# Placing TensorE's side jobs between score fills by the time that ScalarE has in hand

## The chip, the cores and the metric

The kernel runs on one core of a Trainium2 chip. The time is that of one execution on the device, in microseconds (us); the median of several executions stands for a kernel. The engines of a core are TensorE (matmuls, PE in the profile), VectorE (DVE), ScalarE (ACT), GpSimd (POOL) and SyncE (SP), which here only issues transfers.

## The reference

The input x has 2048 positions of 512 features, in bf16. Two attentions with 32 heads of 16 features run on it and are mixed by a gate for each position:

```python
def reference(A_x, A_wqkv, A_wo, B_x, B_wqkv, B_wo, gate_w):
    x = A_x
    g = sigmoid((x * gate_w).sum(-1, keepdims=True))
    a = A_ref(x, A_wqkv, A_wo)   # softmax(q k^T / 4) v over all 2048 keys, then wo
    b = B_ref(x, B_wqkv, B_wo)   # each position sees 8 keys: itself and every second one before it
    return g * a + (1 - g) * b
```

The full attention needs 32 x 2048 x 2048 exponentials, some 134 million. This is what fills the time.

## The kernel before, in words

**Tiles and periods.** The full attention is cut into 32 periods. A period is one chunk of 512 queries for one group of four heads. Within it there are 64 units: one head, 512 queries and one tile of 128 keys. A unit is a matmul of scores (128 keys x 512 queries, one PSUM bank), 65,536 exponentials, and a matmul of the result with V (17 rows, the last of which gives the sum for the softmax) into the accumulator `acc`.

**Where the exponentials are done.** Most units go to ScalarE, in sets that use two PSUM rings in turn: ring A holds three units, ring B two. TensorE fills a ring with scores (`act_stream`, inner `f`: the *fill*, matmuls `ring<-qt,kt_all`), ScalarE turns the whole ring into probabilities with one instruction (`act_tail`: `pT<-ring`), which frees the ring for the fill after next, and TensorE then multiplies by V (`pv_job`: `acc<-pT,vp_all`, called a *V block* here). A fill may carry one or two more units, for which `rider` takes a *job bank* `w`: VectorE computes their exponential with a polynomial in four passes (`dve_unit`: `ta<-w`, twice `ta<-ta,w`, `pd<-ta,w`), or it copies them out and GpSimd computes it (`pool_unit`, tiles `psc`). `idle_fill` can also place such a unit alone, by `solo`.

**Jobs.** All else that TensorE does goes into the two job banks too: projections for queries, keys and values (`q_job`, `k_job`, `kpk_job`, `qpk_job`, `v_job`), the projections and transposes of the sliding attention (`b_proj`, `b_attn`, whose arithmetic is on GpSimd), transposes of finished accumulators (`post_job`, `ot_job`) and the output projections (`final_job`). Most are four matmuls of 512 columns. For 24 of the 32 periods the queries go by way of memory: `qpk_job` projects them, VectorE and GpSimd finish them, a transfer writes them, and `q_read` reads them back two periods ahead of use.

**The order.** The program is written by a planner, class `Plan`, while the kernel is built. It keeps a clock for each engine (`free`), a list of work that is ready (`ready`, with priority, earliest start, the generator, duration, function, bank needed, and in place 7 the time at which it became ready) and the free slots of banks and buffers. It always takes the engine that can start first, and of that engine's ready work that with the lowest priority number: fills have 0, V blocks just over 1, jobs from 2 on. What it picks is issued at once, so the planner's order is the order of each engine's instructions; each engine then runs in order, and only semaphores decide the times. The planner's durations are constants in the code (`MM` 0.22, `SW` 0.11 and `VP` 0.60 us, and 0.050 + 0.4267 us a unit for ScalarE).

**What holds a job back.** A job that would start at `st` must pass `fits`. It does so if it ends before ScalarE, by the planner's clock, has worked off what is ready for it, less a margin `refill`, or if it has waited longer than `patience`:

```python
        if x[0] < 2 or st - x[7] > self.patience or self.spent:
            return True
        lim = max(self.free["act"], st) + sum(y[4] for y in self.ready["act"]) - self.refill
        return st + x[4] <= lim or self.free["act"] + 3.0 < st
```

A set gets into `ready["act"]` only once `act_tail` has a probability buffer (`pTA` and `pTB`, two of each). `rider` gives VectorE no second unit (`flying`) while a job with a near due time is ready.

**Filler.** Where TensorE would be idle for long, `fill_pass` adds matmuls with zero weights, which add zero (`acc<-ident,z`), and a fill may be written twice (*doubled fill*), so that TensorE stays active.

All instructions are recorded through one wrapper, so nearly all carry its line, L292, and are told apart by their tiles.

Of the kernel before, what the change touches and what calls it, by code (L numbers as in the profile page):

```python
# [51 lines left out]
class Plan:  # L52
# [13 lines left out]
    held = {"job": 0}  # L66
    streamed = deque()
    cap_job = 2
    refill = 0.56
    patience = 6.0  # L70

    def resource(self, name, n):
# [97 lines left out]
    def gate(self, need):  # L170
# [6 lines left out]
            return None  # L177
        return min(x[0] for x in self.slots[need])

    def fits(self, x, st):  # L180

        if x[0] < 2 or st - x[7] > self.patience or self.spent:
            return True
        lim = max(self.free["act"], st) + sum(y[4] for y in self.ready["act"]) - self.refill
        return st + x[4] <= lim or self.free["act"] + 3.0 < st

    def run(self):
        while True:
            best = None
            for e, lst in self.ready.items():  # L190
                rs = []
                for x in lst:
                    g_ = self.gate(x[6])
                    if g_ is not None:
                        rs.append(max(x[2], g_))
                if rs:
                    st = max(self.free[e], min(rs))
                    if best is None or st < best[0]:
                        best = (st, 1, e)
            for r, lst in self.reqs.items():  # L200
                if lst and self.slots[r]:
                    st = max(min(x[0] for x in self.slots[r]), min(x[2] for x in lst))
                    if best is None or st <= best[0]:
                        best = (st, 0, r)
            if best is None:
                return
            st, kind, nm = best
            self.now = st
            if kind == 0:
                lst = self.reqs[nm]  # L210
                x = min(y for y in lst if y[2] <= st + 1e-9)
                lst.remove(x)
                s = min(y for y in self.slots[nm] if y[0] <= st + 1e-9)
                self.slots[nm].remove(s)
                self.advance(x[3], st, s[1])
            else:
                lst = self.ready[nm]
                ok = [y for y in lst if y[2] <= st + 1e-9 and self.gate(y[6]) is not None
                      and self.gate(y[6]) <= st + 1e-9]
                x = min(ok, key=lambda y: (y[0], y[1]))  # L220
                if nm == "pe" and not self.fits(x, st):
                    for y in ok:
                        y[2] = max(y[2], st + 0.1)
                    continue
                lst.remove(x)
                if nm == "pe":
                    self.idle_fill(st, 1 + (x[6] is not None))
                if x[6] is not None:
                    slot = self.take(x[6], st)
                    self.held["job"] += 1  # L230
                    more = x[5](slot)
                else:
                    more = x[5]()
                if isinstance(more, float):
                    x[4] += more
                if nm == "pe":
                    self.stream(st, x[4] - 0.11 - self.thin)
                    self.thin = 0.0
                if CFG_DEBUG:
                    LOG.append((st, x[4], nm, getattr(x[3], '__name__', '?'), x[0]))  # L240
                self.free[nm] = st + x[4]
                self.advance(x[3], st + x[4] + self.LAT[nm], None)
# [3 lines left out]
def kernel(  # L246
# [141 lines left out]
    P = Plan(["pe", "act", "dve", "pool", "sp"])  # L388
# [21 lines left out]
    UR = 0.7  # L410
# [37 lines left out]
    NP = len(periods)  # L448
# [328 lines left out]
    front = [0]  # L777
# [11 lines left out]
    flying = [0]  # L789
# [125 lines left out]
    def act_tail(k, parts, rname, rslot, ring, n):  # L915
        pname = "pTA" if k % 2 == 0 else "pTB"
        pslot = yield ("acq", pname, k)
        st = {}

        def f():  # L920
            st["pT"] = work.tile([128, 3 if k % 2 == 0 else 2, QW], BF16, name="pT", tag=pname, bufs=2)
            A.activation(out=st["pT"][:, 0:n, :], in_=ring[:, 0:n, :], func=ACT.Exp,
                         scale=LN2 / 128.0, bias=-VOFF * LN2 / 128.0)
        yield ("act", k, 0.050 + 0.4267 * n, f)
        yield ("rel", rname, rslot)
        pT = st["pT"]
        off = 0
        for q_, (p, us) in enumerate(parts):
            items = [(t, j, pT[:, off + z, :]) for z, (t, j) in enumerate(us)]
            off += len(us)  # L930
            yield ("spawn", pv_job(p, items, (pname if q_ == len(parts) - 1 else "none", pslot), 1 + 1e-4 * k))

    def act_stream():
        while front[0] < NP:
# [5 lines left out]
            units, parts, used = [], [], []  # L940
# [17 lines left out]
            for p_, us in parts:  # L958
                yield ("wait", ev_q[p_])
                for t, j in us:  # L960
                    yield ("wait", ev_k[periods[p_][1]][t // TPC])
                if ev_start[p_].time is None:
                    yield ("set", ev_start[p_])
            ring = ps.tile([128, 3 if k % 2 == 0 else 2, QW], FP32, tag=rname, bufs=1, name="ring")
            dur = SW + MM

            def f():
# [20 lines left out]
                    ndve[0] += 1  # L988
                return float(more)
            yield ("pe", 0, dur, f)  # L990
            yield ("spawn", act_tail(k, parts, rname, slot, ring, len(units)))
        P.spent = True
        yield ("spawn", end_banks("rA", 3))
# [31 lines left out]
    def rider(js, now=None):  # L1025
        now = P.now if now is None else now
        for p in (front[0], front[0] + 1):
# [5 lines left out]
            if not opts:  # L1033
                continue
            j = max(opts, key=lambda j_: len(pend[p][j_]))
            if flying[0] and any(x[6] and x[0] < 4.0 + 0.3 * min(front[0] + UR, 16.3) for x in P.ready["pe"]):
                return None
            if not P.free_at("w", now):
                return None
# [1 line left out]
            if psc[0] is not None and rem(p) >= PMIN and P.free_at("psc", now):  # L1041
                hs = P.take("psc", now)
                npool[0] += 1
            else:
                if not P.free_at("pd", now) or flying[0] > 1:
                    return None
                flying[0] += 1
                ds = P.take("pd", now)
            act_left[p] -= 1
            act_due[p] -= 1  # L1050
# [3 lines left out]
    def dve_unit(p, t, j, s, ds, wt, n):  # L1054
        lo = wt[:].bitcast(U16).rearrange("p (n two) -> p n two", two=2)[:, :, 0]
        st = {}
        pr = 40 + 1e-3 * n

        def e1():
            st["ta"] = work.tile([128, QW], FP32, name="ta", tag="ta", bufs=2)  # L1060
            V.tensor_scalar(out=st["ta"][:], in0=lo, scalar1=A3, scalar2=None, op0=ALU.mult)

        def e23(a):
            ta = st["ta"]
            V.scalar_tensor_tensor(out=ta[:], in0=ta[:], scalar=a, in1=lo, op0=ALU.add, op1=ALU.mult)
        yield ("dve", pr, VP, e1)
# [1 line left out]
        yield ("dve", pr, VP, lambda: e23(A1))  # L1068

        def e4():  # L1070
            st["pd"] = work.tile([128, QW], BF16, name="pd", tag=f"pd{ds}", bufs=1)
            V.scalar_tensor_tensor(out=st["pd"][:].bitcast(U16), in0=st["ta"][:], scalar=A0 - VOFF / 2.0,
                                   in1=wt[:], op0=ALU.add, op1=ALU.add)
# [553 lines left out]
```

## Time and profile before

| | |
|---|---|
| median of 11 runs | 867.49 us (865.93 to 871.87) |
| profiled execution | 865.93 us, of it 864.1 us from the first to the last instruction |
| ScalarE | 835.8 us busy (97%) |
| TensorE matmuls | 753.3 us (87%), weight loads 267.8 us beside them |
| VectorE, GpSimd | 751.1 us and 750.4 us (87% each) |
| `pT<-ring` on ScalarE | 721 instructions, 823.3 us busy, 12.6 us idle before them |
| units on VectorE and GpSimd | 224 and 22 of 2048 |
| first and last exponential | start at 19.17 us, end at 854.26 us |

A row of the profile names the engine, the operation, the tiles written and read with their shapes, the count, the busy time and the mean length of one in ns, and last the idle time of the engine ahead of it with what ended that. The busy time of a group is a union: instructions that overlap are counted once. TensorE's records overlap, since matmuls are pipelined.

### The profile page before, as it was taken

The page shows a single profiled execution, that of the slowest core. Times are in us where ns is not written, and L with a number is a line of the kernel's source. Part 1 is how long each engine was busy: PE and PEld are TensorE (multiplying, and loading weights), DVE is VectorE, ACT ScalarE, POOL GpSimd, SP SyncE. Part 2 cuts the span into 40 slices and gives each one's busy share as a digit, 9 for nine tenths or more (in the row PEclk, how much of TensorE's full clock was granted, in tenths as well). Part 3 has the DMA queues.
Part 4 walks back from the last instruction along what each step waited for, and adds up shares of the span by engine and source line. Part 5 has one row for each costly group of instructions (what it writes and reads, how often), then busy time and mean ns, then how long its engine had stood idle before and what let it go on. Part 6 is the DMA issues. An engine that isn't in the chain of part 4 may idle for free.

```text
span 864.1 us, 16034 instructions
## 1 busy us (share of the span) xinstructions
PE 753.3 (87%) x5977; PEld 267.8 (31%) x6038; DVE 751.1 (87%) x1312; ACT 835.8 (97%) x753; POOL 750.4 (87%) x758
## 2 busy tenths in 40 slices
PE   8898998898988888888898998888888988888887
PEld 4333342243223333332323232323232323223222
DVE  5696889999999989989999889889988889998884
ACT  5999999999999999999999999999999999999996
POOL 2586995999898989999999999998989999978883
PEclk9999999999999999999999999999999999999999
DMA  9000424422215131221042322303022230010000
GB/s 293 2 2 25 136 62 121 147 69 88 96 55 172 31 111 50 80 68 42 7 136 61 92 73 75 104 8 111 1 62 68 84 124 7 25 45 7 1 2 25
DMA packets 55712, 59.79 MB, mean 69 GB/s; under 512 B 3649, under 2 KB 52289, under 8 KB 55633
## 3 DMA queue, kind: packets, MB, share of 16 engines
q1 hardware_dynamic: 54816, 58.50, 21.5%
q8 instruction: 47, 0.77, 0.4%
q10 hardware_dynamic: 816, 0.26, 0.1%
q14 instruction: 33, 0.26, 0.1%
HBM read 46.14 MB, written 12.62 MB: 68 GB/s over the span
## 4 chain that ended last, share of the span: by engine, by line
ACT 51%; issue 20%; PE 18%; DVE 9%; POOL 1%; another core or an unknown queue 0%; ACTq 0%; DVEq 0%; POOLq 0%
ACT pT L292 50%; PE w L292 6%; PE ring L292 6%; PE acc L292 5%; DVE ta L292 4%; DVE pd L292 1%; POOL psc L292 1%; ACT lg L292 1%; DVE kpk L292 1%; PE last L292 1%; PE heat L292 1%; DVE kmax_pk L292 1%; PE xt L292 0%; DVE crow L292 0%; ACT xT L292 0%
## 5 line engine op out<-in xcount | busy, mean ns | idle before, releaser
L292 ACT ACTIVATE pT<-ring 128x1536 bf16<-128x1536 f32 (+1 forms) x721 | 823.3, 1308 | 12.6 <-PE ring L292 8.2
L292 PE MATMUL ring<-qt,kt_all 32*128 32x512 bf16 x1874 | 289.5, 382 | 92.6 <-ACT pT L292 79.8
L292 DVE SCALAR_TENSOR_TENSOR ta<-ta,w 128x512 f32<-128x512 f32 x448 | 297.8, 682 | 5.9
L292 POOL TENSOR_TENSOR prod<-prod 128x512 f32<-128x512 f32 (+1 forms) x208 | 240.1, 1166 | 6.0
L292 PE MATMUL acc<-pT,vp_all 128*17 128x512 bf16 x1802 | 224.6, 384 | 0.1
L292 PEld LDWEIGHTS <-kt_all 32*128 32x128 bf16 x2120 | 107.0, 91 | 335.2 <-issue 317.6
L292 DVE TENSOR_SCALAR ta<-w 128x512 f32<-128x512 uint16 x224 | 151.6, 685 | 37.5 <-PE w L292 36.7
L292 PE MATMUL acc<-ident,z 128*32 128x512 bf16 (+4 forms) x717 | 161.3, 338 | 2.0 <-DVE accS L292 1.8
L292 DVE SCALAR_TENSOR_TENSOR pd<-ta,w 128x512 uint16<-128x512 f32 x224 | 150.8, 680 | 2.7
L292 POOL TENSOR_TENSOR prod<-ksh,qb 128x512 f32<-128x512 bf16 x128 | 145.0, 1156 | 2.1
L292 POOL TENSOR_TENSOR prod<-vsh,lg 128x512 f32<-128x512 bf16 x128 | 136.6, 1098 | 2.4
L292 PE MATMUL w<-qt,kt_all 32*128 32x512 bf16 x246 | 89.9, 383 | 0.1
L292 POOL TENSOR_TENSOR psc<-psc 128x512 f32<-128x512 f32 x66 | 78.8, 1193 | 5.2
L292 PE MATMUL acc<-pd,vp_all 128*17 128x512 bf16 x246 | 80.2, 383 | 0.0
L292 PEld LDWEIGHTS <-z 128*32 128x32 bf16 x742 | 49.7, 95 | 76.3 <-issue 58.4
L292 PEld LDWEIGHTS <-vp_all 128*17 128x17 bf16 x2048 | 43.8, 88 | 85.2 <-issue 82.4
L292 POOL TENSOR_SCALAR psc<-psc 128x512 f32<-128x512 uint16 (+1 forms) x44 | 27.2, 619 | 34.0 <-DVE psc L292 31.1
L292 PE MATMUL w<-bw,xT 128*128 128x512 bf16 x161 | 47.5, 381 | 3.3 <-issue 0.5
L292 PEld LDWEIGHTS <-xT 128*128 128x128 bf16 x512 | 31.2, 97 | 34.7 <-issue 22.3
L292 POOL TENSOR_TENSOR lg<-lg,mx 128x256 f32<-128x256 f32 x16 | 10.1, 629 | 23.2 <-DVE mx L292 23.2
L292 DVE CAST kvs<-w 128x512 bf16<-128x512 f32 x32 | 22.0, 686 | 5.8 <-PE w L292 5.8
L292 DVE COPY accS<-acc 128x512 f32<-128x512 f32 (+1 forms) x32 | 21.6, 675 | 4.4 <-ACT accS L292 4.0
(115 smaller groups left out, 494.1 us busy)
## 6 DMA issues: line engine op xcount, KB each, us to landing
ksh<-kv_scr SPq DMA_DIRECT2D x16, 1024.0 KB
vsh<-kv_scr SPq DMA_DIRECT2D x16, 1024.0 KB
kv_scr<-kvs SPq DMA_DIRECT2D x16, 256.0 KB
kt_all<-k_scr SPq DMA_DIRECT2D x6, 512.0 KB
q_scr<-qpk SPq DMA_DIRECT2D x24, 128.0 KB
qt<-q_scr SPq DMA_DIRECT2D x24, 128.0 KB
xr<-in_A_x_dram SPq DMA_DIRECT2D x4, 512.0 KB
out_dram<-osb SPq DMA_DIRECT2D x14, 128.0 KB
```

Of the source, the lines that this page charges most:

```text
L292: return chain_on(self._key, f(*a, **k))
```

## The change

`fits` no longer lets a job through because of its age. The limit moves to a function of its own, `limit`, which also counts `coming`: the planned ScalarE time of sets that are filled and whose `act_tail` still waits for a probability buffer (added after a fill is issued, taken off when the buffer is had). `refill` goes from 0.56 to 0.5. A job that has waited over `CALM` = 4 us may pass the limit by `RAMP` = 0.02 of the wait beyond that.

In all periods but the first and the last (`calm`) a job for a job bank is put off by 0.1 us at a time, up to `JP` = 3 us, while VectorE has less than `JW` = 1.6 us of work: what it has begun, the queued work of jobs, and 0.6 us for each pass of a unit still to come (`passes`). In `rider` a ready job keeps a second unit from VectorE only if VectorE has that much work. `feed_dve` and the branch on `DEFER` are added with `HUNG` = 0 and `DEFER` = 0.

```diff
--- before.py
+++ after.py
@@ -66,7 +66,7 @@
     held = {"job": 0}
     streamed = deque()
     cap_job = 2
-    refill = 0.56
+    refill = 0.5
     patience = 6.0
 
     def resource(self, name, n):
@@ -177,12 +177,47 @@
             return None
         return min(x[0] for x in self.slots[need])
 
+    DEFER = 0.0
+    coming = 0.0
+    RAMP = 0.02
+    CALM = 4.0
+
+    def limit(self, st):
+        return max(self.free["act"], st) + sum(y[4] for y in self.ready["act"]) + self.coming - self.refill
+
+    passes = 0
+    calm = False
+    JW = 1.6
+    JP = 3.0
+    HUNG = 0.0
+    ASL = 1.2
+
+    def dve_work(self, st):
+
+        return (max(0.0, self.free["dve"] - st) + 0.6 * self.passes
+                + sum(y[4] for y in self.ready["dve"] if y[0] < 40))
+
+    def room_for_job(self, x, st):
+        return not self.calm or st - x[7] > self.JP or self.dve_work(st) >= self.JW
+
+    def feed_dve(self, st):
+
+        if self.solo is None or not self.calm or self.dve_work(st) >= self.HUNG:
+            return False
+        if max(0.0, self.free["act"] - st) + sum(y[4] for y in self.ready["act"]) + self.coming < self.ASL:
+            return False
+        at = self.solo(self.free["pe"], st + 0.35)
+        if at is None:
+            return False
+        self.stream(at, 0.22)
+        self.free["pe"] = at + 0.33
+        return True
+
     def fits(self, x, st):
 
-        if x[0] < 2 or st - x[7] > self.patience or self.spent:
+        if x[0] < 2 or self.spent or self.free["act"] + 3.0 < st:
             return True
-        lim = max(self.free["act"], st) + sum(y[4] for y in self.ready["act"]) - self.refill
-        return st + x[4] <= lim or self.free["act"] + 3.0 < st
+        return st + x[4] - self.limit(st) <= max(0.0, self.RAMP * (st - x[7] - self.CALM))
 
     def run(self):
         while True:
@@ -218,6 +253,18 @@
                 ok = [y for y in lst if y[2] <= st + 1e-9 and self.gate(y[6]) is not None
                       and self.gate(y[6]) <= st + 1e-9]
                 x = min(ok, key=lambda y: (y[0], y[1]))
+                if nm == "pe" and 1 <= x[0] < 1.5 and st - x[2] < self.DEFER:
+                    jobs = [y for y in lst if y[0] >= 2 and y[4] > 0.5 and y[7] <= st
+                            and self.gate(y[6]) is not None and self.gate(y[6]) <= st + 1e-9]
+                    y = min(jobs, key=lambda y: (y[0], y[1])) if jobs else None
+                    if (y is not None and st + y[4] <= self.limit(st)
+                            and (y[6] != "w" or self.room_for_job(y, st))):
+                        x = y
+                if nm == "pe" and self.feed_dve(st):
+                    continue
+                if nm == "pe" and x[6] == "w" and not self.room_for_job(x, st):
+                    x[2] = max(x[2], st + 0.1)
+                    continue
                 if nm == "pe" and not self.fits(x, st):
                     for y in ok:
                         y[2] = max(y[2], st + 0.1)
@@ -915,6 +962,7 @@
     def act_tail(k, parts, rname, rslot, ring, n):
         pname = "pTA" if k % 2 == 0 else "pTB"
         pslot = yield ("acq", pname, k)
+        P.coming -= 0.050 + 0.4267 * n
         st = {}
 
         def f():
@@ -960,6 +1008,7 @@
                 for t, j in us:
                     yield ("wait", ev_k[periods[p_][1]][t // TPC])
                 if ev_start[p_].time is None:
+                    P.calm = 0 < p_ < NP - 1
                     yield ("set", ev_start[p_])
             ring = ps.tile([128, 3 if k % 2 == 0 else 2, QW], FP32, tag=rname, bufs=1, name="ring")
             dur = SW + MM
@@ -988,6 +1037,7 @@
                     ndve[0] += 1
                 return float(more)
             yield ("pe", 0, dur, f)
+            P.coming += 0.050 + 0.4267 * len(units)
             yield ("spawn", act_tail(k, parts, rname, slot, ring, len(units)))
         P.spent = True
         yield ("spawn", end_banks("rA", 3))
@@ -1033,7 +1083,7 @@
             if not opts:
                 continue
             j = max(opts, key=lambda j_: len(pend[p][j_]))
-            if flying[0] and any(x[6] and x[0] < 4.0 + 0.3 * min(front[0] + UR, 16.3) for x in P.ready["pe"]):
+            if flying[0] and (not P.calm or P.dve_work(now) >= P.JW) and any(x[6] and x[0] < 4.0 + 0.3 * min(front[0] + UR, 16.3) for x in P.ready["pe"]):
                 return None
             if not P.free_at("w", now):
                 return None
@@ -1045,6 +1095,7 @@
                 if not P.free_at("pd", now) or flying[0] > 1:
                     return None
                 flying[0] += 1
+                P.passes += 4
                 ds = P.take("pd", now)
             act_left[p] -= 1
             act_due[p] -= 1
@@ -1057,10 +1108,12 @@
         pr = 40 + 1e-3 * n
 
         def e1():
+            P.passes -= 1
             st["ta"] = work.tile([128, QW], FP32, name="ta", tag="ta", bufs=2)
             V.tensor_scalar(out=st["ta"][:], in0=lo, scalar1=A3, scalar2=None, op0=ALU.mult)
 
         def e23(a):
+            P.passes -= 1
             ta = st["ta"]
             V.scalar_tensor_tensor(out=ta[:], in0=ta[:], scalar=a, in1=lo, op0=ALU.add, op1=ALU.mult)
         yield ("dve", pr, VP, e1)
@@ -1068,6 +1121,7 @@
         yield ("dve", pr, VP, lambda: e23(A1))
 
         def e4():
+            P.passes -= 1
             st["pd"] = work.tile([128, QW], BF16, name="pd", tag=f"pd{ds}", bufs=1)
             V.scalar_tensor_tensor(out=st["pd"][:].bitcast(U16), in0=st["ta"][:], scalar=A0 - VOFF / 2.0,
                                    in1=wt[:], op0=ALU.add, op1=ALU.add)
```

## The prediction

> **What bounds the kernel now.** I read the page's busy shares first, then ScalarE's group row, then its waits, then its busy time by stage, and at last one waiting place in the timeline. The busy shares name the engine:
>
> ```profile
> span 864.1 us, 16034 instructions
> PE 753.3 (87%) x5977; PEld 267.8 (31%) x6038; DVE 751.1 (87%) x1312; ACT 835.8 (97%) x753; POOL 750.4 (87%) x758
> ACT 51%; issue 20%; PE 18%; DVE 9%; POOL 1%; another core or an unknown queue 0%; ACTq 0%; DVEq 0%; POOLq 0%
> L292 ACT ACTIVATE pT<-ring 128x1536 bf16<-128x1536 f32 (+1 forms) x721 | 823.3, 1308 | 12.6 <-PE ring L292 8.2
> L292 PE MATMUL ring<-qt,kt_all 32*128 32x512 bf16 x1874 | 289.5, 382 | 92.6 <-ACT pT L292 79.8
> ```
>
> ScalarE is busy 97% of the span, nearly all of it in 721 exponentials of score sets. The last row shows that TensorE, on the whole, waits for ScalarE (79.8 us), so there is room on TensorE; but ScalarE also waits for TensorE, 12.6 us ahead of those exponentials. By form they are 360 of 1536 columns (mean 1.520 us) and 361 of 1024 (1.098 us); that sums to 942.9 us against 823.3 us of busy time, so neighbours overlap by 119.6 / 720 = 0.166 us. A gap costs its idle time and that overlap. By stage (the columns are TensorE, weight loads, VectorE, ScalarE, GpSimd):
>
> ```profile
> 100.00:200.00 100.00, 90.53 (x746) 35.58 (x755) 90.55 (x160) 98.06 (x89) 86.66 (x89) 1.00 0.32 96
> ...
> 200.00:300.00 100.00, 87.87 (x681) 30.07 (x684) 92.00 (x163) 98.25 (x88) 92.62 (x90) 1.00 0.29 94
> ...
> 700.00:800.00 100.00, 84.31 (x687) 29.21 (x686) 92.47 (x161) 99.01 (x90) 87.92 (x87) 0.98 0.13 41
> ```
>
> Over all stretches from 20 to 830 us ScalarE is idle 810.00 - 800.38 = 9.62 us. Its timeline has 41 gaps over 60 ns there. So all that better placing of TensorE's work can win is 9.6 + 41 x 0.166 = 16.4 us, 1.9%. What makes a gap is seen at 466 us:
>
> ```profile
> 464.22 0.60 PE L292 MATMUL acc<-pT,vp_all 128*17 128x512 bf16 x5
> ...
> 464.76 1.04 PE L292 MATMUL w<-bwo,obt 128*128 128x512 bf16 x4
> ...
> 465.73 0.39 PE L292 MATMUL ring<-qt,kt_all 32*128 32x512 bf16 x3
> ...
> 466.23 1.45 ACT L292 ACTIVATE pT<-ring 128x1536 bf16<-128x1536 f32 x1 [0.50 <-PE ring L292]
> ```
>
> A probability-times-V block (0.54 us from 464.22 to 464.76), then a job of four matmuls (0.97 us to 465.73), and only then the score fill, which ScalarE has been waiting for; the exponential starts 0.50 us after its fill. Of the 41 gaps, 35 (7.0 of 9.4 us that they sum to) have such a job just ahead of the late fill. That is what the planner's `fits` is to prevent.
>
> **What the Trainium skill says.** ScalarE: Activation LUTs, "What ACT_TABLE_LOAD costs", gives an ACTIVATE 186 or 280 ns (immediate or pointer bias) plus 0.833 ns a column, so 1466 or 1560 ns at 1536; the trace has 1520, in between. It lets neighbours overlap by about 93 ns; the trace has 166, which I use. PSUM — Partial Sum Buffer, "Specifications (TRN2)", gives 8 banks of 512 FP32 values; the program's two rings (3 + 2), two job banks and one accumulator use all 8, so no third ring can absorb a late fill, and a fill must come in the time of one exponential. The trace agrees in that fills wait for ScalarE 244 times. TensorE: Matmul & The Clock Gate, "What's actually happening", has the clock at half rate after an idle window of about 3.4 us. The trace shows a dip to 0.66 at 620 to 625 us and at 743 to 748 us, and in each one gap (0.58, 0.76 us) in which plain fills were slow, not jobs.
>
> **The change part by part.** All is decided when the program is built; what reaches the chip is another order, which can be counted in the two programs.
>
> *Rule for jobs* (`limit`, `fits`). Before, a job that had waited 6 us went in whatever it delayed; after, it may exceed the limit by 2% of its wait beyond 4 us, 0.04 us at 6 us. In return `coming` adds sets whose fill is issued and which wait for a probability buffer, and the margin falls from 0.56 to 0.50, so jobs are also allowed sooner. I count the work between one score fill and the next in TensorE's order, each block at its traced time (job 0.97, V blocks 0.32 to 0.54). Gaps with over 1.3 us: 46 before, 15 after (0.33). Neighbouring gaps with over 2.0 us together: 56 and 18 (0.32). Gaps with a full job and a V block: 37 and 17 (0.46). Jobs in two neighbouring gaps: 11 and 5. The first two measure excess work itself, so I take 0.33 of the gaps to remain. From the 16.4 us I take the two clock dips, 1.34 + 2 x 0.166 = 1.7: 14.7 us remain, and 0.67 of that is **9.8 us won**; with 0.46 it is 7.9, with everything gone 16.4.
>
> *Holding of jobs while VectorE has work* (`calm`, `room_for_job`, the test in `rider`). VectorE takes 225 units in place of 224, GpSimd 19 in place of 22, ScalarE 1804 in place of 1802 in 722 exponentials. ScalarE pays 2 x 823.3 / 1802 = **0.9 us**, on the path. VectorE gets 4 passes more and 3 copies less, all of 0.60 us by their starts: +0.6 us under its 10% idle time. GpSimd loses 3 x (3 x 1.19 + 3 x 0.62) = 16 us, off the path. A held job delays its banks' readers on VectorE and its chain behind; nothing on the chip waits on an added semaphore. DMAs stay at 155 on SP and none is added.
>
> *Dead parts.* `DEFER` is 0 and `dve_work` is never below `HUNG` = 0, so the deferral and `feed_dve` do nothing: no cost.
>
> *TensorE.* 25 score matmuls fewer (doubled fills go from 30 to 20) and 33 weight loads of filler more; it has 13% idle time, no cost.
>
> *Head.* Before, a V job stood ahead of the first query's correction; now it stands behind the first two fills, with filler in its place. The first fill waited for qt on VectorE and still will (0.1 us gain at most). But the first V block now follows the fifth fill, so the fifth exponential, which needs the first one's buffer, may wait: I take 0 to 0.3 us loss, inside the next figure.
>
> *Tail.* The last exponential has one 512-column unit, and the last V block six matmuls, two deep instead of one: one more pass of 0.22 us. **0.2 us lost**; the bound is -0.5 to +1.
>
> Sum: -9.8 + 0.9 + 0.2 = -8.7 us. The profiled execution took 865.93 us (span 864.1, 1.8 us around it), so 857.2 by its own time; the median of the runs shown lies 1.56 us above it, and I give the number against the median: **858.8 us**.
>
> **The rivals.**
> *VectorE takes over part of the waiting.* TensorE takes a bank only when VectorE has emptied it; in the trace this costs it about 7 us, in gaps such as DVE pd 2.1 and DVE accS 2.0. With VectorE's queue kept fuller (its busy share is already 92% in two stages) these waits may grow and delay fills. Against: all its long passes take 0.60 us, the very cost in the planner. If half of the 9.8 comes back: 863.7.
> *It does nothing measurable*: gaps that the planner doesn't see, by clock and semaphore, make up most of them. Against: 35 of 41 have a job ahead. About 867.
> *Slower, by a late chain.* Held jobs delay the query chain (job, VectorE, GpSimd, two DMAs) so that the first fill of a period waits for qt. 24 periods are fed by it; it decides from (9.8 - 1.1) / 24 = 0.36 us at each. At 0.7 us each: 867.49 - 8.7 + 16.8 = 875.6. Against: such waits are 0.4 us in all now, and in the new order the twelve query jobs stand within 5 fills of their old places (fills 67, 71, 123, 147, 207 for 65, 69, 121, 143, 211), some 5 us, with reads issued two periods ahead. The sliding branch's last transpose moves from fill 666 to 678 of 722, still 44 fills ahead of the end.
>
> **How the numbers follow.** A run of this kernel can tell about 0.2% (1.7 us) from no change. Main case 0.73 (854 to 862); VectorE waiting 0.18 (861 to 866, mostly faster); nothing 0.05; slower by the chain 0.04. Faster 0.92, same 0.04, slower 0.04. The low end is near the case that nearly all gaps go (867.49 - 16.4 + 1.1 = 852.2); the high end takes in half of the gain coming back.
>
> **What would show it.** Right: ScalarE's idle time from 20 to 830 us at 3 to 5 us in place of 9.6; pT x722; the row's wait for PE ring near 4 us, 2.9 of them at the start; no job ahead of most remaining gaps. Wrong: idle time of 8 us or more there, or new waits of TensorE's jobs for DVE ta, DVE pd, or of ring for qt. If the time falls by over 15 us, the gaps were worth more than I count.

## The result, and the profile after

| | before | changed |
|---|---|---|
| median | 868.28 us (50 runs, 865.86 to 872.46) | 861.42 us (13 runs, 857.6 to 866.33) |
| profiled execution | 865.93 us | 862.72 us |
| span of it | 864.1 us | 860.9 us |
| start of the first exponential | 19.17 us | 19.23 us |
| from there to the end of the last exponential | 835.09 us | 830.19 us |
| from there to the end of the span (the tail) | 9.86 us | 11.51 us |

The changed kernel takes 0.9921 of the time before (interval 0.9906 to 0.9937). It is 6.9 us faster; 8.7 us were forecast. From here on, "after" is the changed kernel.

These are the same parts of the page in the same order: the busy shares, the chain that ended last, ScalarE's group of exponentials and TensorE's group of fills.

```profile
span 860.9 us, 16027 instructions
PE 753.2 (87%) x5989; PEld 271.1 (31%) x6044; DVE 749.6 (87%) x1313; ACT 833.5 (97%) x754; POOL 734.5 (85%) x740
ACT 66%; issue 21%; PE 10%; DVE 2%; DMA 1%; SPq 0%; ACTq 0%
L339 ACT ACTIVATE pT<-ring 128x1536 bf16<-128x1536 f32 x722 | 822.2, 1384 | 9.9 <-PE ring L339 6.0
L339 PE MATMUL ring<-qt,kt_all 32*128 32x512 bf16 x1849 | 288.9, 384 | 89.5 <-ACT pT L339 75.1
```

The shares of busy time say nothing: ScalarE stays at 97%. The chain says more. ScalarE makes up 66% of it in place of 51%, TensorE 10% in place of 18%, VectorE 2% in place of 9%: the path leaves ScalarE less often. The exponentials' idle time goes from 12.6 to 9.9 us, and the part that waits for a fill from 8.2 to 6.0 us.

By stage (columns: stretch, its length, then the busy time and count of TensorE, weight loads, VectorE, ScalarE and GpSimd, then the granted clock of TensorE, DMA share and GB/s), the three stretches shown for before and the one from 20 us read:

```profile
20.00:100.00 80.00, 73.42 (x647) 26.27 (x653) 58.61 (x101) 76.05 (x68) 49.89 (x56) 0.94 0.10 32
100.00:200.00 100.00, 92.05 (x766) 35.93 (x773) 90.60 (x160) 100.00 (x91) 92.16 (x96) 1.00 0.32 102
200.00:300.00 100.00, 87.91 (x676) 30.98 (x677) 92.02 (x163) 99.72 (x91) 92.72 (x91) 1.00 0.29 91
...
700.00:800.00 100.00, 84.79 (x685) 30.06 (x687) 91.15 (x158) 99.89 (x91) 87.05 (x84) 1.00 0.15 46
```

From 100 to 200 us, the densest stretch for jobs, ScalarE is now busy without a break, with 91 instructions in place of 89. Most of what is lost early (2.8 of 3.95 us) is lost in the half clock behind the 0.94 of the clock column. From 20 to 830 us ScalarE is idle 6.9 us in place of 9.62; its timeline has 20 gaps of over 60 ns there in place of 41, and 3.9 us of the new sum lie in moments with the clock at half.

The place where the prediction showed a late fill, the job `w<-bwo,obt` near 466 us, looks like this in the timeline of after (start, length, engine, operation):

```profile
463.46 5.96 ACT L339 ACTIVATE pT<-ring 128x1536 bf16<-128x1536 f32 x5
...
465.06 0.39 PE L339 MATMUL ring<-qt,kt_all 32*128 32x512 bf16 x3
...
465.38 1.04 PE L339 MATMUL w<-bwo,obt 128*128 128x512 bf16 x4
...
466.35 0.39 PE L339 MATMUL ring<-qt,kt_all 32*128 32x512 bf16 x2
```

The job now follows a fill directly, with no V block between that fill and the next. ScalarE runs five exponentials through it from 463.46 to 469.42 us.

**A second profile of after.** A profile of one execution has its own dips of the clock. Run e14 is the changed kernel once more, and its profile is the quieter one (granted clock 0.996; before's profile has 0.995).

> The changed kernel itself beside the last one: ratio to before 0.991 to 0.994, and the same time at equal clock as when it was first measured (about 858.8 at a clock of 0.995).

Its median was 860.5 us, ratio 0.9913 (0.9882 to 0.9944), 859.3 us at clock 0.995: as expected. These are its span and its group of exponentials, and then two lines of its waits (engine, tile, what it waited for; sum, times, longest in us):

```profile
span 857.7 us, 16027 instructions
...
L339 ACT ACTIVATE pT<-ring 128x1536 bf16<-128x1536 f32 x722 | 821.6, 1379 | 6.8 <-PE ring L339 3.8
```

```profile
ACT osc L339 <- DVE osb L339: 5.9, 1, 5.9
...
ACT pT L339 <- PE ring L339: 3.8, 3, 2.9
```

ScalarE's wait for fills is down to 3.8 us, of which 2.9 us is the wait for the very first fill; ScalarE's idle time from 20 to 830 us is 3.9 us in 15 gaps. The exponentials take 826.30 us from the first to the last. The other line, a wait of 5.9 us at the very end, is new (before's longest there is 4.2 us), and comes up again below.

### The profile page after: what moved, and what is told of

Read it like the earlier page. It is cut to its first block, busy times and chain, and to the rows that moved or that the text cites. A ratio compares the mean times of both kernels' runs of the same rounds, so it can differ in the third digit from the quotient of the medians.

```text
span 860.9 us, 16027 instructions
## 1 busy us (share of the span) xinstructions
PE 753.2 (87%) x5989; PEld 271.1 (31%) x6044; DVE 749.6 (87%) x1313; ACT 833.5 (97%) x754; POOL 734.5 (85%) x740
## 4 chain that ended last, share of the span: by engine, by line
ACT 66%; issue 21%; PE 10%; DVE 2%; DMA 1%; SPq 0%; ACTq 0%
ACT pT L339 64%; PE ring L339 3%; PE w L339 3%; PE acc L339 3%; ACT lg L339 1%; DVE ta L339 1%; PE last L339 1%; DMA xr<-in_A_x_dram 1%; PE xt L339 0%; ACT xT L339 0%; DVE kmax_pk L339 0%; DVE xT L339 0%; DVE kpk L339 0%; DVE pd L339 0%; ACT osc L339 0%
## 5 line engine op out<-in xcount | busy, mean ns | idle before, releaser
L339 ACT ACTIVATE pT<-ring 128x1536 bf16<-128x1536 f32 x722 | 822.2, 1384 | 9.9 <-PE ring L339 6.0
L339 PE MATMUL ring<-qt,kt_all 32*128 32x512 bf16 x1849 | 288.9, 384 | 89.5 <-ACT pT L339 75.1
L339 DVE SCALAR_TENSOR_TENSOR ta<-ta,w 128x512 f32<-128x512 f32 x450 | 302.1, 682 | 6.5
L339 PEld LDWEIGHTS <-kt_all 32*128 32x128 bf16 x2093 | 111.5, 91 | 332.9 <-issue 316.6
L339 DVE TENSOR_SCALAR ta<-w 128x512 f32<-128x512 uint16 x225 | 153.6, 686 | 41.5 <-PE w L339 39.0
L339 PE MATMUL acc<-ident,z 128*32 128x512 bf16 (+4 forms) x745 | 166.6, 338 | 2.4 <-DVE accS L339 2.0
L339 PE MATMUL w<-qt,kt_all 32*128 32x512 bf16 x244 | 92.8, 386 | 0.2 <-DVE pd L339 0.2
L339 PEld LDWEIGHTS <-z 128*32 128x32 bf16 x775 | 51.7, 95 | 73.7 <-issue 53.6
L339 POOL TENSOR_TENSOR psc<-psc 128x512 f32<-128x512 f32 x57 | 68.0, 1193 | 4.4
L339 POOL TENSOR_SCALAR psc<-psc 128x512 f32<-128x512 uint16 (+1 forms) x38 | 23.5, 618 | 43.5 <-DVE psc L339 35.8
```

Of the source, the lines that this page charges most:

```text
L339: return chain_on(self._key, f(*a, **k))
```

## The experiments

All variants are of the changed kernel. Two measures of the order stand beside the times; both are counted in the program as in the prediction: **pairs**, neighbouring spaces between fills with over 2.0 us of work together, and **adjacent jobs**, jobs in two neighbouring spaces. ScalarE's gaps (over 60 ns, from 20 us to the end of the exponentials) and the tail come from each kernel's own profile. Since the granted clock differs from run to run, and with it the time by some 0.5 us for each 0.001 (see the last section), the last column sets each kernel's runs to the clock 0.995 by a straight line through them; it is an estimate of mine, good to about 1 us. If an order draws fewer dips by itself, the ratio has that in it and this column hasn't: the mean clock of the runs is 0.990 for before and after, and 0.994 to 0.996 for e1, e4 and e11.

| kernel | median us | ratio to before | pairs | adjacent jobs | gaps, us | tail us | us at clock 0.995 |
|---|---|---|---|---|---|---|---|
| before | 868.28 | 1 | 56 | 11 | 41, 9.4 | 9.86 | 866.2 |
| after | 861.42 | 0.9921 (0.9906–0.9937) | 18 | 5 | 21, 7.0 | 11.51 | 858.8 |
| after again (e14) | 860.50 | 0.9913 (0.9882–0.9944) | 18 | 5 | 15, 3.9 | 11.51 | 859.3 |
| e1: no holding | 865.37 | 0.9962 (0.9942–0.9982) | 33 | 15 | 24, 7.8 | 12.35 | 865.0 |
| e2: old rule, with holding | 871.88 | 1.0050 (1.0032–1.0069) | 67 | 18 | 49, 14.2 | 12.34 | 871.8 |
| e3: patience back | 867.40 | 0.9979 (0.9968–0.9990) | 56 | 6 | 42, 7.7 | 12.35 | 866.0 |
| e4: `coming` left out | 863.03 | 0.9949 (0.9933–0.9965) | 26 | 5 | 20, 6.8 | 9.79 | 863.8 |
| e5: two end banks | 858.06 | 0.9888 (0.9858–0.9918) | 18 | 5 | 18, 4.4 | 9.80 | 857.4 |
| e13: the same again | 857.75 | 0.9892 (0.9862–0.9922) | 18 | 5 | 17, 4.1 | 9.79 | 857.6 |
| e8: margin 0 | 867.86 | 1.0003 (0.9990–1.0016) | 53 | 11 | 45, 10.9 | 10.52 | 866.2 |
| e9: margin 0.56 | 869.60 | 1.0010 (0.9990–1.0029) | 31 | 12 | 25, 10.4 | 11.64 | 866.4 |
| e10: margin 0.44, two end banks | 859.33 | 0.9908 (0.9881–0.9936) | 23 | 7 | 21, 5.0 | 9.68 | 858.3 |
| e11: as e10, no holding | 860.81 | 0.9912 (0.9888–0.9936) | 27 | 9 | 20, 7.0 | 10.01 | 861.3 |
| e12: dense filler, two end banks | 880.16 | 1.0135 (1.0105–1.0165) | 63 | 5 | 64, 19.0 | 9.79 | – |

**Which part of the change does it?** The theory of the prediction (A in the expectations) is that fewer late fills behind jobs bring the gain, by the new rule; its rivals are that the holding of jobs does, or neither. The first three runs do one part alone or undo one.

e1, the new rule without the holding:

```diff
-    JW = 1.6
+    JW = 0.0
```

> The new fits without the holding of jobs: JW = 0, so room_for_job always says yes and rider's test is the old one. Its order has 21 gaps over 1.3 us and 33 neighbouring pairs over 2.0 us (before 46 and 56, changed kernel 15 and 18). Theory A, the gain comes from late fills taken away: 0.48 of 14.7 us won, 0.9 us for two units more on ScalarE, 1.6 us for the longer end that the changed kernel has too: 863 to 865, ratio to before about 0.995. Theory B, the gain comes from holding jobs for VectorE: no gain left, 868 to 870, ratio 1.000 or above.

Measured: 0.9962, a little less than expected. That is half of the gain by the ratio, but only 1.2 of 7.4 us at one clock. The exponentials take 831.41 us from first to last, 3.7 us less than before, and a tail that is 2.5 us longer takes most of that back.

e2, the old rule and margin with the holding:

```diff
-        if x[0] < 2 or self.spent or self.free["act"] + 3.0 < st:
+        if x[0] < 2 or st - x[7] > self.patience or self.spent:
             return True
-        return st + x[4] - self.limit(st) <= max(0.0, self.RAMP * (st - x[7] - self.CALM))
+        lim = max(self.free["act"], st) + sum(y[4] for y in self.ready["act"]) - 0.56
+        return st + x[4] <= lim or self.free["act"] + 3.0 < st
```

> The holding of jobs with the old fits (patience of 6 us, margin 0.56, sets without a buffer not counted). Order: 48 gaps over 1.3 us, 67 pairs over 2.0 us; VectorE and GpSimd take 249 units, ScalarE 1799. Theory A: no late fill is taken away, 1.4 us won by three units fewer on ScalarE, 1.6 us lost at the end, up to 3 us lost by the further pairs: 868 to 871, ratio 1.000 to 1.003. Theory B: 861 to 863, ratio 0.993.

Measured: 1.0050, slower than before and just above the range of theory A. ScalarE's gaps sum to 14.2 us. Held jobs age, and the old rule lets an aged job in whatever it delays. The group of exponentials shows it (before: 12.6 us idle, fills the largest part):

```profile
L340 ACT ACTIVATE pT<-ring 128x1536 bf16<-128x1536 f32 x720 | 822.7, 1311 | 17.3 <-PE w L340 6.9
```

e3, the changed kernel with one clause of before put back:

```diff
-        if x[0] < 2 or self.spent or self.free["act"] + 3.0 < st:
+        if x[0] < 2 or st - x[7] > self.patience or self.spent or self.free["act"] + 3.0 < st:
```

> The changed kernel with one clause put back: a job that has waited over 6 us passes fits whatever it delays. Order: 44 gaps over 1.3 us, 56 pairs over 2.0 us, 249 units off ScalarE. Theory A, with patience as what made fills late: nearly all the gain goes, 866 to 869, ratio 0.998 to 1.001, and ScalarE's idle time from 20 to 830 us back to 8 to 10 us. Rival C, the gain comes from counting the coming sets and the smaller margin: 861 to 863, ratio 0.993.

Measured: 0.9979, a quarter of the gain by the ratio and 0.2 us of 7.4 at one clock. There are 42 gaps (before has 41), and the 56 pairs are back. Its group of exponentials:

```profile
L339 ACT ACTIVATE pT<-ring 128x1536 bf16<-128x1536 f32 x720 | 822.3, 1325 | 10.9 <-PE ring L339 4.8
```

Not all of the loss is late fills, though: the exponentials still take 3.3 us less than before (831.79 us), and a tail of 12.35 us, 2.5 us longer than before's, takes most of that back. Of the time that jobs cost ScalarE, about four fifths of what the change saves are back (10.7 us, with 12.7 before and 3.3 in after; the table under "The margin" has them). So the one clause that lets a job in by its age decides over most of the gain. Orders built for other margins, which did not run, agree by their pairs: with the clause and all else, margins from 0.44 to 0.56 give 48 to 58 pairs; without it, margins from 0.40 to 0.60 give 18 to 42 with holding and 27 to 38 without.

**Is `coming` needed?** e4:

```diff
-        return max(self.free["act"], st) + sum(y[4] for y in self.ready["act"]) + self.coming - self.refill
+        return max(self.free["act"], st) + sum(y[4] for y in self.ready["act"]) - self.refill
```

> The changed kernel with coming left out of limit, so sets that wait for a probability buffer are not counted; no patience, margin 0.5. Order: 25 gaps over 1.3 us, 26 pairs over 2.0 us (changed kernel 15 and 18, before 46 and 56), 242 units off ScalarE; the last set is in ring A, as before, so the end should be the short one (about 10 us). Theory A (taking patience away is what counts): half of 14.7 us won, 1.8 us lost on ScalarE: 861 to 864, ratio 0.993 to 0.996. Rival C (counting the coming sets is what counts): 866 to 868, ratio 0.998 to 1.000.

Measured: 0.9949, as theory A expected. Some 5 us of the gain at one clock go with `coming`, though the tail is short here. Two more units stay on ScalarE (242 in place of 244 are done elsewhere), and 2.8 us are lost at one place, at 131 us, where an exponential waits 2.74 us for a V block that stands behind VectorE's copy of an accumulator. That is one event of one order: whether `coming` is worth 5 us in other orders is not shown.

**The margin.** The rule says a job is late if it ends past the limit; then a margin of 0 should bring late fills, and 0.56 a few less than 0.50. e8 and e9 change that number alone:

```diff
-    refill = 0.5
+    refill = 0.0      # e8
+    refill = 0.56     # e9
```

> The changed kernel with the margin refill at 0 in place of 0.5, so every job may end 0.5 us later against the limit; no patience. Order: 42 gaps over 1.3 us, 53 pairs over 2.0 us, 250 units off ScalarE, last set in ring A. Theory A: a late fill costs the same whichever clause lets it in; 0.9 us won on gaps, 1.8 us on ScalarE's units: 864 to 867, ratio 0.996 to 0.999, with ScalarE's gaps as many as before (35 to 45). Rival D (an age limit matters for itself, by jobs in a bunch, and a margin doesn't): 859 to 862.

> The changed kernel with the margin of before, refill 0.56. Order: 20 gaps over 1.3 us, 31 pairs over 2.0 us, 245 units off ScalarE; last set in ring A (short end). Theory A, with the margin as a choice between near-equal orders: half of 14.7 us won, 0.5 us lost on units: 860 to 863, ratio 0.992 to 0.995. Rival C (the margin and the counting let jobs go in time): 865 or more.

e8 came out at 1.0003, just above the range of theory A: with 53 pairs and 45 gaps all of the gain is gone, so it is the lateness of fills that costs, not age as such.

e9 is a miss: expected faster, measured 1.0010, no gain at all. It has only 25 gaps, but they sum to 10.4 us. A typical one, in the timeline of e9:

```profile
483.26 0.59 PE L339 MATMUL w<-bw,xT 128*128 128x512 bf16 x2
...
483.79 0.39 PE L339 MATMUL ring<-qt,kt_all 32*128 32x512 bf16 x2
...
484.64 1.04 PE L339 MATMUL w<-awo,oT 128*128 128x512 bf16 x4
485.61 0.39 PE L339 MATMUL ring<-qt,kt_all 32*128 32x512 bf16 x3
...
486.11 1.45 ACT L339 ACTIVATE pT<-ring 128x1536 bf16<-128x1536 f32 x1 [0.49 <-PE w L339]
```

Two jobs stand on either side of one fill. The first makes that fill later than it would be, still in time; the second, with V blocks ahead of it (484.11 to 484.64), finds no time left, and the next fill starts 1.82 us after the last, whose two units give ScalarE 0.9 us of work. The order of e9 has 12 jobs in adjacent spaces, after has 5. It also loses time at one place at 833 us, to a V block:

```profile
833.46 1.45 ACT L339 ACTIVATE pT<-ring 128x1536 bf16<-128x1536 f32 x1 [1.68 <-PE acc L339]
```

To see what each order loses and where, I took the ends of the exponentials. With no wait between them they end 1.343 us apart for a set of three units and 0.917 us for one of two, in every kernel here. What an end comes later than that after the one ahead is lost. Each loss from 0.02 us on is sorted by what TensorE did in the space before the fill (a job is three or more of its matmuls there), or put down to the half clock where the granted clock was at half; 4.8 us in which ScalarE does something else between two exponentials, 5.5 in e8, are left out.

| us lost on ScalarE | before | after | after again | e1 | e2 | e3 | e4 | e8 | e9 | e10 | e11 |
|---|---|---|---|---|---|---|---|---|---|---|---|
| a job, with another in the space before it | 5.45 | 0.93 | 0.82 | 4.17 | 8.53 | 2.90 | 1.35 | 3.03 | 4.87 | 0.82 | 2.33 |
| any other job | 7.26 | 2.38 | 2.05 | 2.30 | 7.66 | 7.83 | 3.03 | 7.70 | 1.79 | 2.24 | 2.19 |
| half clock | 1.55 | 4.61 | 1.38 | 2.01 | 2.30 | 1.02 | 1.18 | 2.46 | 1.39 | 1.77 | 3.27 |
| V block, buffer, other | 1.47 | 1.95 | 1.76 | 2.69 | 2.57 | 2.11 | 4.41 | 4.12 | 5.91 | 3.25 | 1.97 |
| all | 15.7 | 9.9 | 6.0 | 11.2 | 21.1 | 13.9 | 10.0 | 17.3 | 14.0 | 8.1 | 9.8 |
| units on ScalarE | 1802 | 1804 | 1804 | 1804 | 1799 | 1799 | 1806 | 1798 | 1803 | 1802 | 1806 |

With 0.43 us for each unit, the sums account for the stretch of exponentials to within 0.2 us in every column: from before to the second profile of after 9.7 us less are lost, two more units cost 0.9 us, and the stretch falls by 8.8 us. The two rows of jobs fall from 12.7 us to 3.3 and 2.9 us. That is the change.

The rows tell two things apart. The second falls from 7.3 us to 1.8 to 3.0 in all seven columns without the age clause and with a margin of 0.44 to 0.56, and stays at 7.7 to 7.8 in e2, e3 and e8, which let jobs in late by age or by margin: this part the rule brings in every order. The first row goes from 0.8 to 4.9 us under the same rule: this part is the luck of the order. Neighbouring jobs are few but costly: of the 23 in before (smaller jobs and transposes counted too), 16 made a fill late; of its other 168 jobs, 39 did.

So e9's forecast failed not by its jobs, which cost 6.0 us less than before where 7.3 were expected. Waits for V blocks and buffers cost 4.4 us more, 1.8 of them in the gap at 833 us, and the end, expected to be short, is 1.8 us longer: there ScalarE's copy of the last accumulator waits 2.1 us for a V block, for 0.8 in before. No term of the forecast had these.

Over the ten orders (one time of after, and neither e5 and e13, whose order differs in the tail alone, nor e12) the time at clock 0.995 less the excess of the tail rises with the pairs, by 0.18 us for each (correlation 0.84), with up to 2.9 us to either side of the line: the rule moves the time, and the luck of one order moves it by 2 to 3 us more.

**The tail.** After's tail is 1.65 us longer than before's, in both profiles. The timelines of before (the first two lines) and of after have this at the end (brackets: idle time ahead, and what ended it):

```profile
856.47 1.24 PE L292 MATMUL last<-bwo,obt 128*128 128x512 bf16 x5
...
859.64 0.58 ACT L292 CAST osc<-last 128x512 bf16<-128x512 f32 x1 [4.18 <-PE last L292]
```

```profile
852.20 0.59 PE L339 MATMUL last<-bwo,obt 128*128 128x512 bf16 x2 [0.27 <-DVE rden L339]
...
853.31 0.59 PE L339 MATMUL last<-bwo,obt 128*128 128x512 bf16 x2 [0.51 <-DVE otok L339]
...
856.44 0.58 ACT L339 CAST osc<-last 128x512 bf16<-128x512 f32 x1 [5.89 <-DVE osb L339]
857.08 0.38 PE L339 MATMUL last<-awo,oT 128*128 128x512 bf16 x1 [1.40 <-ACT osc L339]
```

When the scores end, `end_banks` turns the rings into banks for the last output sums, and those of one ring are one tile `last`. In after the last set lies in ring B, so ring A comes free first, and its three banks take two output sums and the last transpose together. Matmuls to one of its banks then wait for VectorE's reading of another (`rden`, `otok` in the brackets), and ScalarE's copy `osc` for VectorE's `osb`. Before had five of these matmuls in one piece and no such wait. The test gives ring A two banks at the end, so that the transpose goes into the other tile, and leaves the one-unit last set as it is. If the shared tile costs the time, before's tail comes back; if the last set does, it doesn't. e5:

```diff
-        yield ("spawn", end_banks("rA", 3))
+        yield ("spawn", end_banks("rA", 2))
```

> The changed kernel, but only two of ring A's three banks are handed to the last output rows (end_banks of rA with 2 for 3), so that the last transposes and the copies that read them lie in another tile than the two sums of direct_job. Theory: the end is longer than before because all of these share one tile, so matmuls and ScalarE's copy wait for VectorE's readers of another bank; then the time from the end of the last exponential falls from 11.5 us to about 10, and the whole by 1.2 to 1.6 us against the changed kernel: 859.8 to 860.2, ratio to before 0.990 to 0.991. Rival: the end is set by the chain through VectorE and the transfers anyway: 861.4, ratio 0.992, end of 11 to 11.5 us.

The same place in the timeline of e5:

```profile
848.37 1.24 PE L339 MATMUL last<-bwo,obt 128*128 128x512 bf16 x5
...
851.54 0.59 ACT L339 CAST osc<-last 128x512 bf16<-128x512 f32 x1 [4.17 <-PE last L339]
852.18 0.38 PE L339 MATMUL last<-awo,oT 128*128 128x512 bf16 x1 [0.67 <-ACT osc L339]
```

Five matmuls in one piece, no wait between them, and a tail of 9.80 us with the same last set: the tile was to blame. (In e1 to e3 the tail is 0.84 us longer still, by another cause: the last V block, on a unit that ScalarE did not compute, stands behind nine output matmuls, and ScalarE's copy of the accumulator waits 3.09 us for it.) The ratio of e5, 0.9888, is a little better than expected, and was measured again:

> The kernel with two end banks once more, beside the changed kernel on one chip: if only the end differs, it is 1.5 to 1.8 us faster than that at equal clock.

It came to 0.9892 (0.9862 to 0.9922). Beside the changed kernel, measured twice at 0.9921 and 0.9913, the intervals overlap; the 1.7 us are shown by the two tails (9.80 and 9.79 against twice 11.51 us) and by the times at one clock (857.4 and 857.6 against 858.8 and 859.3), not by the ratios. It is the fastest of the versions here.

**Is the holding needed?** With two end banks, two orders at margin 0.44 with and without holding:

```diff
-    refill = 0.5
+    refill = 0.44
-        yield ("spawn", end_banks("rA", 3))
+        yield ("spawn", end_banks("rA", 2))
-    JW = 1.6          # e11 only
+    JW = 0.0
```

> A candidate for a faster version: the changed kernel with two end banks of ring A and the margin at 0.44. Order: 17 gaps over 1.3 us, 23 pairs over 2.0 us, 246 units off ScalarE (two more than the changed kernel, 0.9 us). Theory A: about as fast as the kernel with two end banks alone, 857 to 860, ratio 0.988 to 0.991.

> No holding of jobs (JW = 0), the new fits with a margin of 0.44, two end banks of ring A. Order: 20 gaps over 1.3 us, 27 pairs over 2.0 us (the earlier one without holding, at 0.5, has 21 and 33), 242 units off ScalarE. Theory A': taking patience away brings most of the gain, and holding helps only in that one order at 0.5: 860 to 863, ratio 0.992 to 0.995. Theory B': holding is itself worth about 5 us once patience is gone: 864 to 866, ratio 0.997 to 0.998.

Measured: 0.9908 and 0.9912. The ratios don't differ, but the runs of e11 had the higher clock (mean 0.996, for 0.991 in e10). At one clock e11 is 3 us behind, and between the two profiles, of nearly equal clock (0.994 and 0.993), its exponentials take 3.5 us longer (830.99 and 827.52 us). Four more units on ScalarE are 1.7 us of that, and jobs cost 4.5 us in place of 3.1. So the rule alone takes away most of what jobs cost (12.7 to 4.5 us, and to 6.5 in e1). The holding is not what brings the gain, but in both pairs of orders (e10 and e11, after and e1) it goes with 1.5 to 3.5 us less lost to jobs. Two pairs, where orders scatter by 2 to 3 us, don't settle how much is its own. What `RAMP` does was not tried alone.

**The half clock.** Several fills in after are slow because TensorE runs at half clock, as from 34 to 38 us, where a fill of three is 0.61 us long and not 0.39 (timeline of after):

```profile
36.02 1.02 PE L339 MATMUL acc<-pT,vp_all 128*17 128x512 bf16 x5
36.97 0.61 PE L339 MATMUL ring<-qt,kt_all 32*128 32x512 bf16 x3
```

The exponential behind this fill starts after a gap of 1.26 us. e12 asks whether more filler would pay, with TensorE made busier in thin moments: a fill is doubled below 0.75 of the planner's measure of recent activity, and filler is added below 0.6:

```diff
-                for _ in range(1 + twice):
+                extra = (shut is not None and not any(row_left[shut])
+                         and P.have(P.now + dur) < 0.75 * P.HAM)
+                for _ in range(1 + extra):
...
+                elif (shut is not None and any(row_left[shut])
+                        and P.have(P.now + dur) < 0.6 * P.HAM):
+                    fill_pass(0.2134, P.now)
```

(with two end banks; the planner is not told of the added time.)

> The kernel with two end banks, with filler that the planner does not count: 19 more doubled fills and 230 more zero matmuls, same units and jobs in the same order. By its order no stretch of 3.41 us streams less than half of its time (1.4% of all stretches in the changed kernel). Theory E: the half-rate clock follows such thin stretches, so the granted clock goes from about 0.990 to 0.997 or more in every run, though the time rises to 870 or more by fills that the filler makes late. Rival: the dips come from elsewhere (power, the chip's phase): the clock stays at 0.985 to 0.995.

Measured: 1.0135. Nearly all dips go: the clock was 0.997, 0.999, 0.997 and 0.999 in its four runs, where the mean of before and of after is 0.990 (the profile has one dip left, at 505 us). But late fills come in their place (group of exponentials and the two groups that it crowds, e12):

```profile
L339 ACT ACTIVATE pT<-ring 128x1536 bf16<-128x1536 f32 x722 | 827.5, 1285 | 22.5 <-PE ring L339 16.2
L339 PE MATMUL ring<-qt,kt_all 32*128 32x512 bf16 x1894 | 290.4, 382 | 41.7 <-ACT pT L339 34.3
L339 DVE TENSOR_SCALAR ta<-w 128x512 f32<-128x512 uint16 x225 | 153.8, 686 | 56.7 <-PE w L339 54.7
```

ScalarE waits 16.2 us for fills (6.0 in after), and TensorE's room, the wait for ScalarE ahead of fills, falls from 75.1 to 34.3 us; VectorE waits 54.7 us for units in its banks, for 39.0. Filler that the planner doesn't count costs more than the dips; counted filler was not tried.

## Why the prediction was right, and where it was off

**Bound and kind of gap: right.** The time came out of ScalarE's waits for fills behind jobs (12.7 us lost before, 3.3 and 2.9 after), and putting the age clause back brings most of them back (10.7 us in e3).

**Late fills, −9.8, and two more units, +0.9: right, with a good share of chance.** Together −8.9 for the stretch of exponentials; measured 835.09 to 826.30 us, −8.8, between two profiles of nearly equal clock (0.995 and 0.996). In the first profile it was −4.9, since half clock cost 4.6 us there in place of 1.4. Jobs cost 9.4 and 9.8 us less, the forecast to the tenth, but by two factors that were off against each other: the base was 12.7 us and not 14.7, and a quarter of it stayed and not a third. The price of a gap was off too. All gaps in all profiles cost their idle time and 0.11 us; the 0.166 us is the mean overlap of the records, and more than is lost. That made the sum of 16.4 us too large by 41 x 0.06 = 2.4 us; on the other side it left out delays without idle time, and the ends show 15.7 us lost in all. And e9 shows that counts of spaces price the jobs alone: its 20 spaces over 1.3 us promised that half of what jobs cost would go, half of it went, and other waits and the tail took it back.

**Tail, +0.2: the step that failed.** It measured +1.65, outside its bound of −0.5 to +1, for the waits inside one tile that e5 takes away. I priced the last V block by its passes and did not look at where the last set lies: it decides which ring's banks take the last sums. The waits in between could have been seen in the order (the number of `last` tiles and what shares one).

**Sum.** −8.8 + 1.65 = −7.2 us at one clock, against a measured −6.9 by the medians and −7.4 and −6.9 at clock 0.995 (866.2 to 858.8 and 859.3). The miss of 1.8 us against the forecast of −8.7 is the tail, near enough (1.45 us).

**Holding and head: as forecast.** TensorE's waits for VectorE ahead of a job bank fell from 5.8 to 1.5 us; VectorE stays at 87% busy and GpSimd goes from 87% to 85%. The first exponential starts at 19.23 and 19.84 us for 19.17, within the 18.95 to 19.84 us of all profiles here, so the head shows nothing. Of the marks, idle time of 3 to 5 us was 3.9 in the second profile but 6.9 in the first, and the wait for fills 3.8 and 6.0 for "near 4": a mark from one profile needs the dips taken off.

**The rivals.** VectorE taking over the waiting did not occur (its part of the chain fell from 9% to 2%). A late query chain did not occur: no wait for `qt` grew. But a slower outcome was nearer than its chance says, by a mechanism that I had not named: the order itself. The same rule with margin 0.56 won nothing, and with the old rule holding lost 0.5%. The margin 0.50 is a good point of a scattered family (18 pairs of 18 to 42), not a typical one.

**Clock.** The prediction took the dips as unchanged. On average they are (mean clock 0.990 before and after), but one execution varies by more than its 1.7 us.

## What to carry to other kernels

Where one engine is the bound and another feeds it in order, ask of each block put between two feeds whether it ends in the time in hand, and don't let one through because it is old: here that clause alone brought 7 to 8 us of late feeds back. Then look for two such blocks in neighbouring spaces: what they cost differed by up to 4 us between orders of one rule, as did the waits for V blocks and buffers. Price a gap by the ends of the bound engine's instructions, not by the overlap of their records. A rule for a greedy planner is worth what a family of orders shows, not what one order does: change a number such as its margin by a tenth and see whether the gain stays. At the end of a program look at which results share a tile with banks still being read.

## What the runs showed of the hardware

- **The clock's grid.** The granted clock's changes to a half and back lie on a fixed grid of 3413 ns in each run, with a phase that differs from run to run. All 24 dips between 25 and 850 us, over 14 profiles, follow a window of that grid in which TensorE's matmuls streamed 0.45 to 0.51 of the time (an estimate from columns at 2.4 a ns: 512 columns start 216 ns apart in before's jobs). A usual window has 0.61. Most windows under 0.50 were not followed by a dip (before has 7 between 60 and 840 us, and 2 dips), so what else decides stays open. The Trainium skill, TensorE: Matmul & The Clock Gate, "What's actually happening", speaks of an idle window; here a window half full was enough.
- **What the clock costs here.** Over 81 runs of before, at clocks from 0.981 to 0.995, the time falls by about 0.5 us for each 0.001 of granted clock, though ScalarE is the bound: a dip makes fills late (0.61 us for a fill of three and not 0.39). Carried on to full clock, as an estimate beyond the runs of before, the lines give 863.8 us before and 856.1 us after.
- **Ends, not starts.** While ScalarE never waits, its exponentials of three units end 1.343 us apart, but their records grow from 1.445 to 1.714 us: the starts run up to 0.27 us ahead. After a wait the record is 1.45 us again. So a gap costs its idle time and 0.107 us (0.106 to 0.109 for each gap of all 14 profiles), whatever the overlap of the records was.
- **Banks of one tile.** In this program sums in different banks waited for each other because they were one tile; 1.7 us at the end (11.51 and 9.80 us).
